# A retention layer and two feed-forward layers on one core: the second tile's state chains merged, rounding and scaled queries moved, two units' loads taken ahead of weights

## The chip, the core and the metric

The kernel runs on 1 core of a Trainium2 chip. The metric is the device time of one execution in microseconds (us). A core has five engines with a queue each: TensorE (PE, its weight load shown apart as PEld), VectorE (DVE), ScalarE (ACT), GpSimd (POOL) and SyncE (SP). Here SP issues nearly all loads; DMAs that add onto their destination are issued by POOL.

## What is computed

```python
def _attn_ref(q, k, v):                      # q, k, v: (2, 8, 768, 64)
    B, H, S, D = q.shape
    gamma = 1.0 - 2.0 ** (-5.0 - np.arange(H, dtype=np.float32))
    scale = 1.0 / np.sqrt(D)
    state = np.zeros((B, H, D, D), dtype=np.float32)
    for t in range(S):
        state = gamma[None, :, None, None] * state + np.einsum('bhd,bhe->bhde', k[:, :, t], v[:, :, t])
        y[:, :, t] = scale * np.einsum('bhd,bhde->bhe', q[:, :, t], state)

def reference(**kwargs):
    x = attn_out.transpose(0, 2, 1, 3).reshape(B * S, H * D)     # 1536 tokens x 512
    x = ((x @ w_a) * (x @ w_b)) @ w_out                          # d_ff 1536
    h = x @ w_in                                                 # d_ff 2048
    return np.maximum(0.01 * h, h) @ moe2_w_out
```

All results are float32. Batch 2, 8 heads, 768 steps, head size 64.

## The kernel before, in words

**Retention.** The 1536 tokens are three tiles of 512. A unit is one tile with one pair of heads, so there are 12 units: 0 to 3 are the first tile, 4 to 7 the second, 8 to 11 the third. Units 0 to 3 work in chunks of 128 steps (the `wide_` functions), the others in chunks of 64, eight to a unit (`subs`). A unit u loads its four tiles n, v (plain k and v) and q, k (transposed). ACT scales n into kd (`scaled_keys`, L584); POOL scales q into qs (`scaled_queries`, L589). PE forms kv per chunk (`states`, L592) and the scores sc (L627); DVE masks sc into P (`masked`, L649) and adds kv chunk by chunk onto the decaying state (`add`, L604): one small instruction per chunk, each of which reads the last one's result. PE then makes x from P and v (`within`) and from qs and the states (`across`). A sequence of 768 steps has 12 chunks of 64, so the second tile holds the last four chunks of one sequence and the first four of the next; the second chain starts with a plain copy (L607) and does not read the first.

**Weights.** They arrive as 64-bit words of 512 KB per 128 rows (`raw_`). ACT begins a rounding in three steps (`begin_steps`, L308 to L312), DVE ends it in three (`round_steps`, L326 to L330). Each rounded float32 tile is split into a high part (ACT, `a0h`) and a low part (DVE subtraction, `a0l`, L961 or L385), and each product of two matrices takes three matmuls (`mm3`, L257 to L259): high by high, high by low, low by high. For each later a-weight the low part is instead made by an ACT multiplication by -1 and a POOL DMA that adds the rounded tile (L382, L383).

**Order.** Every engine runs its own queue strictly in the order in which the source calls it; nothing reorders it. The loop over u (L1021) issues for each u: PE's `states(u + 1)` with `within(u)`, `scores(u + 1)` with `across(u)`, then `FILL[u]` blocks of the first feed-forward layer (`first_blocks`, L964, products pa and pb of weights a0, b0, a1, b1), and between them the DVE, ACT and POOL work. `ROUND` says in which u which weight is rounded, `QUERIES` and `KEYS` in which u scaled queries and keys are issued early, `loads(u + AHEAD)` the loads. `low` (L958) makes the low parts that are pending. `outer` (L983, issued at L1115) is eight DMAs of POOL that add whole tiles xf onto others in two interleaved chains of four; their results feed the casts s10 to s41 (L771).

**Fast blocks.** From f = 2 on, each pair of weight blocks a, b is worked by seven products in place of eight (`seven_for_eight`, L780). It accumulates in a bank named top, from which ACT copies three times (L868, L851, L872) while PE waits to add the next product. Its weights pass through `queue`, which `pump(us)` empties by about so many us at a time. `sub_items` (L400) forms differences of the rounded a and b tiles on DVE.

Of the kernel before, what the change touches and what calls it, by code (L numbers as in the profile page):

```python
# [26 lines left out]
NPAIR = H // 2  # L27
# [17 lines left out]
KEYS = {-1: (2,), 0: (3,), 3: (5,)}  # L45
QUERIES = {5: (7, 8), 6: (9, 10), 7: (11,)}
# [183 lines left out]
def retention_moe_kernel(ctx: ExitStack, tc: tile.TileContext, ins, out):  # L230
# [109 lines left out]
    queue, spare, behind = [], [], []  # L340

# [51 lines left out]
    def enqueue_next(f):  # L393
        for k in "ab":
            enqueue_round()
            enqueue_split((k, f), f in FAST, k == "a")
# [189 lines left out]
    @known  # L586
    def scaled_queries(u, t, p, d):
        d["qs"] = slots.new(F32, f"qs{u}")
        nc.gpsimd.tensor_mul(by_sub(d["qs"]), by_sub(d["q"]), pair_table(p, 0))  # L589

    @known
    def states(u, t, p, d):  # L592

        kv, own, todo = bank(f"kv{u}"), chain[u % 2], []
        d["own"] = [carry[p][t % 2]] + [own[:, m] for m in range(1, SUB)] + [carry[p][(t + 1) % 2]]
        d["adds"] = []
        for m, c in enumerate(subs):
            at0 = (t * SUB + m) % SPB
            if at0 == SPB - 1:
                continue  # L600
            for r in heads:
                todo.append(((kv[r, c], d["kd"][r, c], d["v"][r, c]), (True, True)))

            def add(c=c, m=m, first=not at0):  # L604
                o = d["own"][m + 1]
                if first:
                    nc.vector.tensor_copy(o, kv[:, c])  # L607
                else:
                    nc.vector.scalar_tensor_tensor(
                        o, d["own"][m], small[:, NPAIR + p:NPAIR + p + 1], kv[:, c], op0=ALU.mult, op1=ALU.add  # L610
                    )

            d["adds"].append(add)
        slots.done(1)
        return todo
# [330 lines left out]
    load_weights()  # L946
# [11 lines left out]
    def low():  # L958
        while lows:
            key = lows.pop()  # L960
            nc.vector.tensor_sub(weights[key][1], rounded.pop(key), as32(weights[key][0]))  # L961
            slots.done(1)
# [33 lines left out]
    def rounding(u):  # L996
        weigh(u)
        if ROUND.get(u + 1, (0, 0, 0))[2] > 1:
            begin_weights()
        while done:  # L1000
            high(done.pop())

    def weigh(u):
        if u not in ROUND:
            return
        kind, f, n = ROUND[u]
        if n > 1:
            turn.append(round_steps())
        for _ in range(n):
            next(turn[0], None)  # L1010
        if ROUND.get(u + 1, (0, 0))[:2] != (kind, f):
            for _ in turn.pop():
                pass
            done.append((kind, f))
# [5 lines left out]
    turn = []  # L1020
    for u in range(-1, len(units)):  # L1021
        if u < NPAIR:
# [14 lines left out]
            else:  # L1037
                masked(u + 1)
                weigh(u)
                for step in un[u + 1]["adds"][:3]:  # L1040
                    step()
# [15 lines left out]
            if u == NPAIR - 1:  # L1057
                high(done.pop())
                low()
                for step in un[u + 1]["adds"][3:]:  # L1060
                    step()
                x_low(u)
# [5 lines left out]
        else:  # L1068
# [3 lines left out]
            steps = un[u + 1]["adds"] if u + 1 in un else []  # L1072
            if u == NPAIR:
                weigh(u)
                masked(u + 1)
                for step in steps:
                    step()
                x_high(u)
                keys(u + 2)
                queries(u + 2)  # L1080
                high(done.pop())
                low()
                x_low(u)
                begin_weights()
            else:
                low()
                for step in steps[:3]:
                    step()
                masked(u + 1)
                for step in steps[3:4]:  # L1090
# [5 lines left out]
                for step in steps[4:]:  # L1096
# [8 lines left out]
        loads(u + AHEAD)  # L1105
        if u in (10, 11):
# [48 lines left out]
    for f in range(NBLOCK, FF1):  # L1155
# [26 lines left out]
        if before:  # L1182
            next(before, None)
            make_products(f - 1)
        if f == FAST[-1]:
# [371 lines left out]
```

## Time and profile before

| what | value |
|---|---|
| median of 3 runs | 563.97 us (563.68 to 564.5) |
| the profiled execution's own time | 563.54 us |
| its span | 561.7 us |
| PE busy | 551.4 us, 98% of the span |
| DVE, ACT, POOL busy | 463.3, 386.8, 155.3 us |

The span runs from the first to the last instruction of the profile; the 1.84 us beside it lie around it. The PE's busy time counts a matmul from its start to its modelled end, so a stall shows as PE idle time, and a lower clock shows as longer matmuls under a granted clock below 1.00.

### The profile page before, as it was taken

Reading aid. Unit: us, or ns where it says so; the run is one execution under the profiler, and the core shown is the slowest. Engines: PE = TensorE matmul, PEld = TensorE weight load, DVE = VectorE, ACT = ScalarE, POOL = GpSimd, SP = SyncE. Lnnn points to the kernel's source line nnn. Section 1 sums busy time; section 2 is a strip of 40 time slices with the busy share of each in tenths; the row PEclk is TensorE's granted clock in tenths of the full one; section 3 lists DMA queues with packets and bytes.
Section 4 is the critical chain, followed back from the end, with each engine's and each line's share of the span. In section 5 each row is a group of like instructions: output and inputs, shape, how many; then the busy total and the mean of one; then the engine's idle time right before and its main releaser. Section 6 shows DMA issues by size and latency. Waiting matters only on the chain.

```text
span 561.7 us, 10490 instructions
## 1 busy us (share of the span) xinstructions
PE 551.4 (98%) x3745; PEld 462.8 (82%) x3745; DVE 463.3 (82%) x984; ACT 386.8 (69%) x796; POOL 155.3 (28%) x198
## 2 busy tenths in 40 slices
PE   8899998999999999999999999999999999999997
PEld 5777886888888888888888888888888888888886
DVE  5888966888988898999769887896977798999862
ACT  4865466777887888968747556778766896678800
POOL 2240320113223231157540140221333467600000
PEclk9999999999999999999999999999999999999999
DMA  8994744548887889699993361764677799964111
GB/s 317 394 388 176 144 76 116 145 140 231 229 214 212 252 224 301 197 333 233 248 223 96 57 131 39 215 178 157 194 254 229 213 273 238 226 159 121 57 57 57
DMA packets 50053, 108.78 MB, mean 194 GB/s; under 512 B 5968, under 2 KB 13392, under 8 KB 50000
## 3 DMA queue, kind: packets, MB, share of 16 engines
q1 hardware_dynamic: 27504, 66.86, 35.7%
q0 software_dynamic: 22208, 40.91, 34.1%
q8 instruction: 29, 0.48, 0.3%
q10 hardware_dynamic: 288, 0.34, 0.2%
q14 instruction: 24, 0.20, 0.1%
HBM read 74.00 MB, written 18.35 MB: 164 GB/s over the span
## 4 chain that ended last, share of the span: by engine, by line
PE 85%; DMA 10%; ACT 2%; DVE 1%; issue 1%; POOL 0%; SPq 0%; POOLq 0%
PE blk L258 12%; PE blk L257 12%; PE blk L259 12%; PE top L257 5%; PE top L258 5%; PE top L259 5%; DMA xf<-xf 3%; PE pa L259 3%; PE pa L257 3%; PE pa L258 3%; PE pb L259 3%; PE pb L258 3%; PE pb L257 3%; PE mid L257 3%; PE mid L258 3%; PE mid L259 3%
## 5 line engine op out<-in xcount | busy, mean ns | idle before, releaser
L258 PE MATMUL blk<-form,form 128*128 128x512 f32 (+1 forms) x224 | 75.8, 339 | 0.0
L257 PE MATMUL blk<-form,form 128*128 128x512 f32 (+1 forms) x224 | 75.6, 337 | 0.0
L259 PE MATMUL blk<-form,form 128*128 128x512 f32 (+1 forms) x224 | 75.3, 336 | 0.0
L173 DVE TENSOR_TENSOR form<-g,form 128x512 fp32r<-128x512 f32 x112 | 57.7, 553 | 0.9
L258 PE MATMUL blk<-forma,forma 128*128 128x512 f32 (+1 forms) x168 | 56.9, 338 | 0.0
L257 PE MATMUL blk<-forma,forma 128*128 128x512 f32 (+1 forms) x168 | 56.7, 337 | 0.0
L259 PE MATMUL blk<-forma,forma 128*128 128x512 f32 (+1 forms) x168 | 56.4, 336 | 0.0
L167 ACT CAST form<-g 128x512 fp32r<-128x512 f32 x112 | 52.6, 514 | 3.6 <-DMA g<-g 2.2
L173 DVE TENSOR_TENSOR forma<-h,forma 128x512 fp32r<-128x512 f32 x84 | 43.1, 554 | 5.4 <-ACT forma L167 3.9
L257 PEld LDWEIGHTS blk<-form,form 128*128 128x128 f32 x224 | 42.5, 190 | 5.3
L258 PEld LDWEIGHTS blk<-form,form 128*128 128x128 f32 x224 | 42.5, 190 | 4.7
L259 PEld LDWEIGHTS blk<-form,form 128*128 128x128 f32 x224 | 42.3, 189 | 4.7
L167 ACT CAST forma<-h 128x512 fp32r<-128x512 f32 x84 | 38.9, 512 | 6.5 <-DMA h<-h 6.1
L728 POOL DMA_DIRECT2D farg<-g x26 | 15.7, 617 | 82.4 <-ACT g L1299 62.2
L146 POOL DMA_DIRECT2D h<-h x33 | 32.6, 1161 | 16.4 <-DVE h L858 5.1
L257 PEld LDWEIGHTS blk<-forma,forma 128*128 128x128 f32 x168 | 31.9, 190 | 4.0
L258 PEld LDWEIGHTS blk<-forma,forma 128*128 128x128 f32 x168 | 31.9, 190 | 3.6
L259 PEld LDWEIGHTS blk<-forma,forma 128*128 128x128 f32 x168 | 31.7, 189 | 3.6
L173 DVE TENSOR_TENSOR form<-wq,form 128x256 fp32r<-128x256 f32 x56 | 23.5, 420 | 10.0 <-ACT form L167 9.9
L728 POOL DMA_DIRECT2D farh<-h x19 | 11.0, 576 | 73.5 <-DVE h L858 36.9
L167 ACT CAST form<-wq 128x256 fp32r<-128x256 f32 x56 | 22.7, 405 | 7.4 <-PE blk L258 2.5
L146 POOL DMA_DIRECT2D g<-farg x22 | 22.0, 1059 | 7.2 <-DVE form L173 3.4
(3059 smaller groups left out, 1687.1 us busy)
## 6 DMA issues: line engine op xcount, KB each, us to landing
raw_wi<-in_w SPq DMA_DIRECT2D x16, 512.0 KB, 4.2
raw_wq<-in_w SPq DMA_DIRECT2D x16, 512.0 KB, 5.3
farg<-g POOLq DMA_DIRECT2D x26, 256.0 KB, 3.9
g<-farg SPq DMA_DIRECT2D x26, 256.0 KB, 6.6
raw_a<-in_wab SPq DMA_DIRECT2D x12, 512.0 KB, 5.0
raw_b<-in_wab SPq DMA_DIRECT2D x12, 512.0 KB, 5.3
raw_wo<-in_wo SPq DMA_DIRECT2D x12, 512.0 KB, 5.1
g<-farg POOLq DMA_DIRECT2D x20, 256.0 KB, 8.0
```

The source lines that it names most:

```text
L146: queue.append((0.0, lambda piece=piece: self.nc.gpsimd.dma_start(self.A(*d[1:], j)[piece], self.A(*x1[1:], j)[piece], accum_op=ALU.add)))
L167: nc.scalar.copy(h, src)
L173: nc.vector.tensor_sub(*todo.pop(0))
L257: nc.tensor.matmul(ps, w[0], x[0], start=first, stop=False, skip_group_check=more)
L258: nc.tensor.matmul(ps, w[0], x[1], start=False, stop=False, skip_group_check=more)
L259: nc.tensor.matmul(ps, w[1], x[0], start=False, stop=last, skip_group_check=more)
L728: nc.gpsimd.dma_start(self.far[t, f], self.tiles[t, f])
```

## The change

What it does, part by part:

1. Loads: the weight tile that stood ahead of each of units 5 and 6 on SP's queue, and likewise of unit 7, now stands behind that unit's four loads.
2. States of the second tile (units 4 to 7): the chunk steps 1 and 2 of both chains are one instruction each (`both`, 128x2x64), seven instructions become five; for units 6 and 7 the copy that starts the second chain moves from DVE to ACT.
3. Around unit 4 the whole chain is done ahead of the mask, and the rounding of weight a0 behind it; the rounding of b0 moves behind unit 5's chain; the low parts of x03 and x20 move ahead of those of a0 and b0.
4. Unit 5: kd5 moves up on ACT between the first and the second step that begin a0; qs5 is made by DVE in the midst of the rounding of a0, no longer by POOL.
5. Each later query scaling on POOL waits for the last low part that was issued ahead of it (a0l, b0l, a1l, b1l), and units 8 and 10 are one u later in `QUERIES`.
6. The low part of a2 is a DVE subtraction, no longer an ACT step and a POOL DMA; so the eight sums `outer` are the first DMAs on POOL.
7. At the first fast block `pump(2.0)` runs the roundings of a3 and b3 ahead of the copies out of top and left.

```diff
-KEYS = {-1: (2,), 0: (3,), 3: (5,)}
-QUERIES = {5: (7, 8), 6: (9, 10), 7: (11,)}
+KEYS = {-1: (2,), 0: (3,)}
+QUERIES = {5: (7,), 6: (8, 9), 7: (10, 11)}
...
-            enqueue_split((k, f), f in FAST, k == "a")
+            enqueue_split((k, f), f in FAST, k == "a" and f in FAST[1:])
...
     def scaled_queries(u, t, p, d):
         d["qs"] = slots.new(F32, f"qs{u}")
-        nc.gpsimd.tensor_mul(by_sub(d["qs"]), by_sub(d["q"]), pair_table(p, 0))
+        args = by_sub(d["qs"]), by_sub(d["q"]), pair_table(p, 0)
+        if u == NPAIR + 1:
+            nc.vector.tensor_mul(*args)
+            return
+        made = nc.gpsimd.tensor_mul(*args)
+        if behind_low:
+            tc.add_manual_dep(
+                made.ins, behind_low[-1].ins.name,
+                mybir.DependencyInfo(mybir.DependencyClass.Sync, mybir.DependencyReason.DATA),
+            )
...
     def states(u, t, p, d):
...
+        def one(m):
+            add(d["own"][m + 1], d["own"][m], of[:, m])
+
+        def both(m):
+            add(own[:, m + 1::fresh][:, :2], own[:, m::fresh][:, :2], of[:, m::fresh][:, :2])
+
+        fresh = -t * SUB % SPB
+        if fresh < SUB:
+            copy = nc.vector.tensor_copy if u < NPAIR + 2 else nc.scalar.copy
+            d["copy"] = lambda: copy(own[:, fresh + 1], of[:, fresh])
+            todo_adds = [lambda: one(0)]
+            todo_adds += [lambda m=m: both(m) for m in range(1, fresh - 1)]
+            todo_adds += [lambda m=m: one(m) for m in range(2 * fresh - 1, SUB)]
+        else:
+            d["copy"] = lambda: None
+            todo_adds = [lambda m=m: one(m) for m in range(SPB - 1 - t * SUB % SPB)]
...
     loads(4)
     load_weights()
-    load_weights()
     loads(5)
     load_weights()
     loads(6)
...
         while lows:
             key = lows.pop()
-            nc.vector.tensor_sub(weights[key][1], rounded.pop(key), as32(weights[key][0]))
+            behind_low.append(
+                nc.vector.tensor_sub(weights[key][1], rounded.pop(key), as32(weights[key][0]))
+            )
...
     def rounding(u):
         weigh(u)
         if ROUND.get(u + 1, (0, 0, 0))[2] > 1:
-            begin_weights()
+            for n, _ in enumerate(begin_steps()):
+                if not n and u == NPAIR - 2:
+                    keys(NPAIR + 1)
...
             else:
+                un[u + 1]["copy"]()
+                for step in un[u + 1]["adds"]:
+                    step()
                 masked(u + 1)
-                weigh(u)
-                for step in un[u + 1]["adds"][:3]:
-                    step()
+                rounds = weigh_steps(u)
+                next(rounds)
+                next(rounds)
+                queries(NPAIR + 1)
+                next(rounds, None)
...
             if u == NPAIR - 1:
                 high(done.pop())
+                x_low(u)
                 low()
-                for step in un[u + 1]["adds"][3:]:
-                    step()
-                x_low(u)
                 begin_weights()
...
+            mid = len(steps) // 2
+            if steps and u > NPAIR:
+                un[u + 1]["copy"]()
             if u == NPAIR:
-                weigh(u)
                 masked(u + 1)
+                un[u + 1]["copy"]()
                 for step in steps:
                     step()
                 x_high(u)
                 keys(u + 2)
                 queries(u + 2)
+                weigh(u)
                 high(done.pop())
+                x_low(u)
                 low()
-                x_low(u)
                 begin_weights()
...
         loads(u + AHEAD)
+        if u < 0:
+            load_weights()
...
         if before:
             next(before, None)
             make_products(f - 1)
+        else:
+            pump(2.0)
```

PE's order is unchanged, instruction by instruction. In the rows below a name's first number is the unit or the weight (kv4, a0), the numbers behind it are buffers.

VectorE, unit 4 and weight a0, before:

```order
L651 TENSOR_TENSOR P4_73_462<-sc4_445,second_76 128x512
L326 TENSOR_SCALAR a0_68_408<-a0_68_408 128x512
L328 TENSOR_SCALAR a0_68_408<-a0_68_408 128x512
L330 ISA a0_68_408<-a0_68_408,sl0_409 128x1024
L609 SCALAR_TENSOR_TENSOR cr0_85<-ca01_78,second_76,kv4_430 128x64
L609 SCALAR_TENSOR_TENSOR cr0_85<-cr0_85,second_76,kv4_430 128x64 x2
L961 TENSOR_TENSOR a0l_79_486<-a0_68_408,a0h_78_485 128x512
L607 COPY cr0_85<-kv4_430 128x64
L609 SCALAR_TENSOR_TENSOR cr0_85<-cr0_85,second_76,kv4_430 128x64 x2
L609 SCALAR_TENSOR_TENSOR ca00_77<-cr0_85,second_76,kv4_430 128x64
L662 TENSOR_TENSOR x03l_75_479<-x3_421,x03h_74_478 128x512
```

and now:

```order
L625 COPY cr0_85<-kv4_432 128x64
L614 SCALAR_TENSOR_TENSOR cr0_85<-ca01_78,second_76,kv4_432 128x64
L614 SCALAR_TENSOR_TENSOR cr0_85<-cr0_85,second_76,kv4_432 128x2x64 x2
L614 SCALAR_TENSOR_TENSOR ca00_77<-cr0_85,second_76,kv4_432 128x64
L670 TENSOR_TENSOR P4_74_469<-sc4_447,second_76 128x512
L326 TENSOR_SCALAR a0_68_408<-a0_68_408 128x512
L328 TENSOR_SCALAR a0_68_408<-a0_68_408 128x512
L592 TENSOR_TENSOR qs5_75_473<-q5_23_158,second_76 128x512
L330 ISA a0_68_408<-a0_68_408,sl0_409 128x1024
L681 TENSOR_TENSOR x03l_77_485<-x3_423,x03h_76_484 128x512
L980 TENSOR_TENSOR a0l_79_488<-a0_68_408,a0h_78_487 128x512
```

The chain of unit 4 (cr0, ca00) now stands whole ahead of the mask P4, in five instructions; qs5 is new, inside the rounding of a0, and x03l stands ahead of a0l.

SyncE, the loads of units 5 and 6 (n, v, q, k) and the weight tiles, before:

```order
L287 DMA raw_a0_152<-in_wab 128x512
L287 DMA raw_b0_154<-in_wab 128x512
L507 DMA n5_21_156<-in_kn 128x512
L507 DMA v5_22_158<-in_vn 128x512
L507 DMA q5_23_160<-in_qT 128x512
L507 DMA k5_24_162<-in_kT 128x512
L287 DMA raw_a1_164<-in_wab 128x512
L507 DMA n6_25_166<-in_kn 128x512
L507 DMA v6_26_168<-in_vn 128x512
L507 DMA q6_27_170<-in_qT 128x512
L507 DMA k6_28_172<-in_kT 128x512
```

and now:

```order
L287 DMA raw_a0_152<-in_wab 128x512
L508 DMA n5_21_154<-in_kn 128x512
L508 DMA v5_22_156<-in_vn 128x512
L508 DMA q5_23_158<-in_qT 128x512
L508 DMA k5_24_160<-in_kT 128x512
L287 DMA raw_b0_162<-in_wab 128x512
L508 DMA n6_25_164<-in_kn 128x512
L508 DMA v6_26_166<-in_vn 128x512
L508 DMA q6_27_168<-in_qT 128x512
L508 DMA k6_28_170<-in_kT 128x512
```

raw_b0 stands behind unit 5 and raw_a1 behind unit 6.

ScalarE at the first fast block, around the first copy out of top (h02), before:

```order
L868 COPY h02_165_1414<-top_1424 128x512
L308 ACTIVATE a3_168_1439<-raw_a3_727 128x512
L310 ACTIVATE sl6_1440<-raw_a3_727 128x512
L312 ACTIVATE sl6_1440<-raw_a3_727 128x512
L308 ACTIVATE b3_169_1449<-raw_b3_825 128x512
L310 ACTIVATE sl7_1450<-raw_b3_825 128x512
L312 ACTIVATE sl7_1450<-raw_b3_825 128x512
L693 COPY h12_166_1415<-pa_1417 128x256
```

and now:

```order
L714 ACTIVATE h11_164_1401<-pa11_1284 128x256
L308 ACTIVATE a3_168_1415<-raw_a3_719 128x512
L310 ACTIVATE sl6_1416<-raw_a3_719 128x512
L312 ACTIVATE sl6_1416<-raw_a3_719 128x512
L308 ACTIVATE b3_169_1425<-raw_b3_815 128x512
L310 ACTIVATE sl7_1426<-raw_b3_815 128x512
L312 ACTIVATE sl7_1426<-raw_b3_815 128x512
L887 COPY h02_165_1405<-top_1431 128x512
```

The six steps that begin a3 and b3 stand ahead of the copy of top into h02, behind the copy out of pa11.

## Rows read from the trace of the kernel before

**Rows 1.** The page's busy times: us (share of the span) and instructions.
```profile
PE 551.4 (98%) x3745; PEld 462.8 (82%) x3745; DVE 463.3 (82%) x984; ACT 386.8 (69%) x796; POOL 155.3 (28%) x198
```

**Rows 2.** Stretches: start:end, length, busy us (count) of each engine, PE clock, DMA, GB/s.
```profile
25.50:28.90 3.40, 3.38 (x64) 2.98 (x65) 3.12 (x9) 2.10 (x5) 0.65 (x1) 0.51 1.05 393
60.00:80.00 20.00, 20.00 (x258) 16.58 (x257) 15.45 (x35) 7.85 (x15) 6.88 (x8) 1.00 0.70 120
100.00:500.00 400.00, 399.86 (x1955) 337.71 (x1954) 343.36 (x720) 296.18 (x608) 130.08 (x168) 1.00 0.77 203
500.00:561.70 61.70, 58.20 (x334) 50.96 (x332) 43.46 (x96) 28.92 (x75) 0.87 (x1) 1.00 0.23 73
```

**Rows 3.** PE in order of time, 21 to 43 us: start, us, what [idle before <- releaser].
```profile
21.45 0.88 PE L578 MATMUL x<-qs,wk 128*64 128x128 f32 x12
23.86 0.27 PE L645 MATMUL kv<-v,kd 64*64 64x64 f32 x2 [1.54 <-ACT kd L584]
...
25.52 0.37 PE L645 MATMUL sc<-qs,k 64*64 64x64 f32 x2 [0.49 <-POOL qs L589]
...
27.42 0.79 PE L257 MATMUL pa<-x00h,a0h 128*128 128x512 f32 x1
...
31.02 0.27 PE L645 MATMUL kv<-v,kd 64*64 64x64 f32 x2
...
34.36 0.51 PE L259 MATMUL pb<-x00h,b0l 128*128 128x512 f32 x1 [0.70 <-DVE b0l L961]
...
42.48 0.50 PE L259 MATMUL pa<-x00h,a1l 128*128 128x512 f32 x1 [0.24 <-DVE a1l L961]
```

**Rows 4.** The chain that ended last, in order of time: start, us, what.
```profile
14.57 7.49 DMA raw_b<-in_wab
...
60.14 5.17 DMA xf<-xf
...
87.73 3.58 DMA a3l<-a
```

**Rows 5.** ACT in order of time, 20.8 to 23.8 us.
```profile
20.81 0.67 ACT L308 ACTIVATE a<-raw_a 128x512 f32<-128x512 f32 x1
...
22.63 0.56 ACT L657 CAST x03h<-x 128x512 fp32r<-128x512 f32 x1
23.09 0.72 ACT L584 ACTIVATE kd<-n,second 128x512 f32<-128x512 f32 x1
```

**Rows 6.** DVE in order of time: mask P4, chain of unit 4, a0l, b0l.
```profile
21.57 0.69 DVE L651 TENSOR_TENSOR P<-sc,second 128x512 f32<-128x512 f32 x1 [1.40 <-PE sc L645]
...
23.81 0.28 DVE L609 SCALAR_TENSOR_TENSOR cr<-ca,second,kv 128x64 f32<-128x64 f32 x1
24.12 0.60 DVE L609 SCALAR_TENSOR_TENSOR cr<-cr,second,kv 128x64 f32<-128x64 f32 x2
24.64 1.38 DVE L961 TENSOR_TENSOR a0l<-a,a0h 128x512 fp32r<-128x512 f32 x1
...
32.62 1.69 DVE L961 TENSOR_TENSOR b0l<-b,b0h 128x512 fp32r<-128x512 f32 x1
```

**Rows 7.** POOL in order of time: qs5, the DMA for a2l, the last of the outer sums.
```profile
24.18 1.28 POOL L589 TENSOR_TENSOR qs<-q,second 128x512 f32<-128x512 f32 x1 [3.96 <-DMA q<-in_qT]
...
58.88 1.05 POOL L383 DMA_DIRECT2D a2l<-a  x1 [13.05 <-PE kv L645]
...
76.57 0.86 POOL L1115 DMA_DIRECT2D xf<-xf  x1 [2.37 <-DMA xf<-xf]
```

**Rows 8.** ACT at the first fast block: the first copy out of top.
```profile
81.46 0.61 ACT L868 COPY h<-top 128x512 f32<-128x512 f32 x1
```

**Rows 9.** PE at the first fast block: the three products added onto top.
```profile
83.31 0.39 PE L257 MATMUL top<-s20h,tb2h 128*128 128x512 f32 x1
...
87.96 0.50 PE L257 MATMUL top<-s30h,tb2h 128*128 128x512 f32 x1 [0.41 <-ACT u L851]
...
94.38 0.50 PE L257 MATMUL top<-x22h,ta2h 128*128 128x512 f32 x1 [1.84 <-ACT h L872]
```

More of the change, by code (lines that the diff above doesn't have):

```diff
@@ L340, in retention_moe_kernel @@
     queue, spare, behind = [], [], []
+    behind_low = []
     def pump(us):
@@ L595, in states, with add @@
         d["own"] = [carry[p][t % 2]] + [own[:, m] for m in range(1, SUB)] + [carry[p][(t + 1) % 2]]
-        d["adds"] = []
         for m, c in enumerate(subs):
[L598 to L613, printed above, removed]
+            if (t * SUB + m) % SPB < SPB - 1:
+                for r in heads:
+                    todo.append(((kv[r, c], d["kd"][r, c], d["v"][r, c]), (True, True)))
+        of = by_sub(kv)
+        fall = small[:, NPAIR + p:NPAIR + p + 1]
+        def add(o, old, part):
+            nc.vector.scalar_tensor_tensor(o, old, fall, part, op0=ALU.mult, op1=ALU.add)
+        def one(m):
[12 more added lines that the diff above has]
+            todo_adds = [lambda m=m: one(m) for m in range(SPB - 1 - t * SUB % SPB)]
+        d["adds"] = todo_adds
         slots.done(1)
@@ L998, in rounding, with weigh_steps @@
         if ROUND.get(u + 1, (0, 0, 0))[2] > 1:
-            begin_weights()
+            for n, _ in enumerate(begin_steps()):
+                if not n and u == NPAIR - 2:
+                    keys(NPAIR + 1)
         while done:
             high(done.pop())
+    def weigh_steps(u):
+        if u in ROUND:
+            yield from round_steps()
+            done.append(ROUND[u][:2])
     def weigh(u):
[L1004 to L1014, printed above, removed]
+        for _ in weigh_steps(u):
+            pass
     def fill(u):
@@ L1018, in fill @@
             next(dense)
-    turn = []
     for u in range(-1, len(units)):
@@ L1086, in retention_moe_kernel @@
                 low()
-                for step in steps[:3]:
+                for step in steps[:mid]:
                     step()
                 masked(u + 1)
-                for step in steps[3:4]:
+                for step in steps[mid:mid + 1]:
                     step()
@@ L1095, in retention_moe_kernel @@
                 leave_x(u)
-                for step in steps[4:]:
+                for step in steps[mid + 1:]:
                     step()
```

## The prediction

> **What bounds the kernel now.** I read the page's busy times first. PE is busy for 551.4 of 561.7 us [rows 1], so some 10.3 us is all that PE's waits can give back, apart from a low clock. The table of stretches tells where they are: from 100 to 500 us PE idles 0.14 us in 400, and 3.5 us lie in the tail, where outputs leave [rows 2]. The change touches neither. What it can win lies ahead of 100 us, and PE's own order is unchanged there, so the time is the sum of PE's waits and slow stretches. PE in order of time shows them [rows 3]: 1.54 us until kd5 is there, 0.49 until qs5, 0.70 until b0l, 0.24 until a1l. At the first fast block it waits 0.41 us for ACT's second copy out of top and 1.84 for the third [rows 9]. [...] Together: 1.54 + 0.49 + 1.67 + 0.70 + 0.24 + 0.41 + 1.84 = 6.89 us.
>
> **From unit 4 to the first block (before: PE runs from 22.33, where 21.45 + 0.88 ends, to 31.02, where unit 6's states begin [rows 3]).** I rebuild this stretch from durations of rows.
>
> Loads. The queue moves about 390 GB/s here [rows 2], so 256 KB take 0.67 us. raw_b0 lands at 14.57 + 7.49 = 22.06 [rows 4], n5 0.67 behind it at 22.7. With raw_b0 moved behind unit 5, its four tiles land two such steps (1.34 us) earlier: n5 at 21.4, v5 22.1, q5 at 22.8 in place of 24.18, when POOL begins qs5 [rows 7]. raw_b0 lands some 2.7 us later, at 24.8. If the order of issue did not carry through to landing, n5 would stay at 22.7; that is the far bound, 1.3 us worse, and I take the near one, since the queue is full throughout.
>
> kd5. ACT began it at 23.09, behind the three steps for a0 (20.81 to 22.63, so 0.6 each) and x03h [rows 5]. Now it stands behind the first step: 21.4 to 22.1.
>
> P4 and the chain. The mask began at 21.57, the chain only 2.24 us later [rows 6]; now the chain is first. The kv4 group is complete before the 32 score matmuls that end at 21.45; these take about 1.0 (half of the 1.90 us from 25.52 to 27.42 at half clock [rows 3]), so the chain starts near 20.5. A 64-wide step is 0.31 (23.81 to 24.12). The two-chain step of 128 elements is in no row: at least 0.31, at most the 0.62 of two; a 512-wide mask of 0.69 against 0.28 for 64 gives 0.06 more for 64 more elements, so I take 0.37 and the chain is 3 x 0.31 + 2 x 0.37 = 1.67, to 22.2. P4 (0.69) is there at 22.9. PE waits 0.55 in place of 1.54.
>
> qs5. After P4 come two of the three rounding steps (three were 2.24 - 0.61 = 1.63 us, two about 1.0), then qs5 on DVE. POOL took 1.28 [rows 7]; DVE's 128x512 product of the same shape takes 0.69 [rows 6], so it ends near 24.5. PE finishes states and first products 1.15 us after 22.9 and waits 0.45 for it, as against 0.49.
>
> a0. Its last step ends at 25.1, a0h (ACT, about 0.6) at 25.7, a0l at 26.4. That low part took 1.38 us while POOL scaled qs5 from 24.18 on, and b0l 1.69 [rows 6]; I take 0.69 for both, as POOL now waits for them. PE's scores end at 25.5; it waits 0.2 for a0h and 0.2 for a0l, and does the 12 matmuls of pa in 2.8 (18 matmuls from 83.31 to 87.55 are 0.235 each [rows 9]): 28.7.
>
> kd6 is the new wait. Behind a0h ACT has three steps for b0 (1.82), two copies of about 0.5 and kd6 (0.72): 29.2. PE waits 0.5.
>
> So unit 6 begins at 29.2 in place of 31.02: waits of 0.55 + 0.45 + 0.4 + 0.5 = 1.9 replace 1.54 + 0.49 + 1.67 = 3.7, **a gain of 1.8 us**. It rests on the upper clock; see the rivals.
>
> **b0l and a1l.** DVE after a0l: P5 0.61, chain 1.67, rounding of b0 1.63: 30.3. b0h 30.9, b0l 31.6. PE needs it two groups of 1.0 and two matmuls after 29.2, at 31.8. **The 0.70 goes**, with 0.2 to spare. Then DVE stands: unit 6's chain now needs a copy by ACT, queued behind the steps of a1 (30.9 + 1.82) and a tile copy: about 33.5. From there chain, P6, x21l, a product and the rounding of a1 are 4.8 us, a1h 0.6 and a1l 0.69: 39.6. PE needs it at 42.24 - 2.5 = 39.7. **The 0.24 goes** as well, but its cover is 0.1 us; 0.5 us later on ACT and PE waits 0.4.
>
> POOL's queries now wait for low parts. q6 lands six steps of 0.67 behind q5 (k5, raw_b0 for two, n6, v6, q6), at 26.8, after a0l; qs6 is there at 28.1, PE asks for it at 30.2, so it has 2 us to spare. While POOL works, DVE runs mask and chain, which read one operand from PSUM: the chain at 24.12 kept 0.30 a step beside qs5 [rows 6, 7].
>
> **First fast block.** Before, POOL's a2l DMA goes out at 58.88 and the eight sums behind it; the last is issued at 76.57 [rows 7], with 5.17 us a link [rows 4], and ACT can copy top into h02 only at 81.46 [rows 8], after casts that wait for them. Everything behind is late: a3l's DMA goes out at 87.73 and takes 3.58 [rows 4], then DVE's differences and ACT's third copy, which PE awaits until 94.38. Now POOL is free of queries near 47 (qs10 and qs11 behind b1l) and four links end near 68, some 12 us earlier. DVE pays 0.69 for a2l, ACT saves about as much; DVE is busy for 15.45 of the 20 us from 60 to 80 [rows 2], which hides it.
>
> In exchange the copy into h02 stands behind two weights' steps (2 x 1.82). From the end of pa11 PE has 27 matmuls (6.3 us) to the first product that adds onto top (83.31 before); ACT has two half-width copies (about 0.5), the steps 3.64 and the copy 0.61, 4.75 in all: 1.5 us to spare. With PE 2.7 earlier it wants the third copy at 94.38 - 1.84 - 0.41 - 2.74 = 89.4; a3l's DMA can go out by 81, land at 84.6, and differences (four, 1.8) and casts bring the copy to about 88. **0.41 + 1.84 = 2.25 us go.**
>
> **Sum.** 1.8 + 0.70 + 0.24 + 2.25 = 4.99: the profiled 563.54 becomes 558.5. The median of the runs is 0.43 above the profiled run, so **559.0 us** is predicted. From 100 us on PE's load is unchanged, so the lead is kept.
>
> **Rivals.**
> *The clock falls again.* The new waits (0.55, 0.45, 0.4, 0.5) are shorter but closer together. The stretch from 24.5 would again be at 0.51 and cost 1.6, of which the waits for a0 (0.4) and kd6 (0.5) are swallowed: 0.7 worse, 559.7. For it: the clock fell after 2.03 us of idling in pieces. Against: 0.70 at 34.36 and 1.84 at 94.38 did not lower it [rows 3, 9]. [...]
> *The fast block keeps its wait.* The six steps ahead of h02, or a3l's DMA, are later than I set them: 2.25 us come back, 561.2. The spare 1.4 to 1.5 us speaks against it.
> *ACT's copy for unit 6 delays a1.* DVE stands 1.9 us for it; each us beyond costs PE one, up to about 1.5: 560.5.
> *The loads do not come earlier.* They share one full queue: n5 at 22.7, 1.3 us worse, 560.3.
> *Slower: PE stays at the lower clock.* If the frequent short waits keep it there from 24.5 past unit 6's states, 8 to 9 us of full-clock work take twice as long: -5.0 + 8.5 less 0.9 of swallowed waits is +2.6, 566.6. It decides once the low stretch holds over 7 us of such work. Against it: the clock came back after 3.4 us with dense matmuls under way.
>
> **How the numbers follow.** A measurement of this kernel can tell about 0.2%, 1.1 us, from no change. Chances: forecast 0.50, clock 0.18, fast block 0.12, ACT's copy 0.08, loads 0.05, slower 0.04; 0.03 for several of the small losses together, which leaves a time within the 0.2%. All but the last two are faster by over 0.2%; as two losses can meet in the others, I give 0.90 faster, 0.06 same, 0.04 slower. The low end is all 6.89 us less the 0.55 and 0.45 that the chain sets: 558.1, and 0.4 for shorter waits: 557.7. The high end takes in the fast-block rival with 0.4 for a1: 561.6.
>
> **What would show it.** Right: kd5 at about 21.4; unit 6's states near 29.2 with a clock of 1.00 from 24 to 29; a0l and b0l at 0.69; no PE wait at b0l; the eight sums from 47 to 68; no PE wait of over 0.3 at the first fast block. Wrong: a stretch at 0.51 after 24; PE waiting for POOL's qs6 or qs8, for ACT's copy into h02, or for a1l.

## The result, and the profile after

The changed kernel takes **558.6 us** in the median of 6 runs (557.6 to 561.08), the kernel before 563.83 beside it on the same chip (6 runs): ratio 0.9912, interval 0.989 to 0.9934. Run again later it took 558.11 against 563.88, ratio 0.9907 (0.9887 to 0.9927). The forecast was 559.0, with a range of 557.7 to 561.6. The profiled execution took 557.6 us, the shortest of the six; its span is 555.8.

The page's line of busy times (us, share of the span, instructions), against [rows 1], and its chain that ended last by engine:

```profile
PE 549.5 (99%) x3745; PEld 462.3 (83%) x3745; DVE 458.8 (83%) x976; ACT 385.9 (69%) x797; POOL 152.7 (27%) x196
...
PE 95%; DMA 2%; ACT 1%; DVE 1%; issue 0%; POOL 0%; SPq 0%
```

PE's waits in the whole span of the changed kernel (us in total, times, longest); everything behind the first line is 1.3 us. Of the four waits of [rows 3] one is left, at the matmul that waited for qs5 (`sc L664 <- issue`, 0.29 us where it was 0.49; e9's row for the same matmul names DVE's qs); the two of [rows 9] are gone:

```profile
PE warm L957 <- DVE warm L948: 1.2, 1, 1.2
PE sc L534 <- DMA k<-in_kT: 0.3, 1, 0.3
PE sc L664 <- issue: 0.3, 1, 0.3
PE pb L259 <- issue: 0.3, 1, 0.3
PE x L664 <- DVE P L670: 0.2, 1, 0.2
PE sc L534 <- DVE qs L527: 0.2, 1, 0.2
```

Stretches, with the columns of [rows 2]. The granted clock is 1.00 where it was 0.51 before; PE does not idle from 60 to 80 us, and from 100 to 500 us it is as busy as it was:

```profile
22.40:24.50 2.10, 1.90 (x72) 1.60 (x68) 2.03 (x6) 2.10 (x4) 0.00 (x0) 1.00 1.04 394
24.50:27.90 3.40, 3.05 (x72) 2.23 (x69) 3.28 (x8) 2.45 (x6) 0.40 (x1) 1.00 1.05 394
...
60.00:80.00 20.00, 20.00 (x258) 16.60 (x257) 16.96 (x35) 11.29 (x22) 2.58 (x3) 1.00 0.39 78
...
100.00:500.00 400.00, 399.90 (x1964) 338.41 (x1964) 345.01 (x726) 300.09 (x620) 129.57 (x167) 1.00 0.77 201
```

PE in order of time, for [rows 3] and [rows 9]. Where before it stood for kd5, qs5, b0l, a1l and the copies out of top, two short waits are left around unit 5, at 23.52 and 24.96; the one at 46.34 is new:

```profile
23.00 0.33 PE L664 MATMUL kv<-v,kd 64*64 64x64 f32 x4
23.52 0.27 PE L664 MATMUL x<-P,v 64*64 64x64 f32 x2 [0.20 <-DVE P L670]
...
24.96 0.27 PE L664 MATMUL sc<-qs,k 64*64 64x64 f32 x2 [0.29 <-issue]
...
29.58 0.27 PE L664 MATMUL kv<-v,kd 64*64 64x64 f32 x2
...
32.07 0.40 PE L259 MATMUL pb<-x00h,b0l 128*128 128x512 f32 x1
...
39.70 0.39 PE L259 MATMUL pa<-x00h,a1l 128*128 128x512 f32 x1
...
45.69 0.39 PE L258 MATMUL pb<-x00l,b1h 128*128 128x512 f32 x1
46.34 0.39 PE L259 MATMUL pb<-x00h,b1l 128*128 128x512 f32 x1 [0.27 <-issue]
...
80.73 0.39 PE L257 MATMUL top<-s20h,tb2h 128*128 128x512 f32 x1
...
84.81 0.39 PE L257 MATMUL top<-s30h,tb2h 128*128 128x512 f32 x1
...
88.66 0.39 PE L259 MATMUL pa<-x11h,a3l 128*128 128x512 f32 x1
88.89 0.39 PE L257 MATMUL top<-x22h,ta2h 128*128 128x512 f32 x1
```

DVE in order of time, for [rows 6]: the chain stands ahead of P4, its two pair steps take 0.73 together, and the low parts take 0.69, not 1.38 and 1.69:

```profile
21.52 0.27 DVE L614 SCALAR_TENSOR_TENSOR cr<-ca,second,kv 128x64 f32<-128x64 f32 x1
21.82 0.73 DVE L614 SCALAR_TENSOR_TENSOR cr<-cr,second,kv 128x128 f32<-128x128 f32 x2
22.59 0.28 DVE L614 SCALAR_TENSOR_TENSOR ca<-cr,second,kv 128x64 f32<-128x64 f32 x1
22.78 0.68 DVE L670 TENSOR_TENSOR P<-sc,second 128x512 f32<-128x512 f32 x1
...
26.15 0.69 DVE L980 TENSOR_TENSOR a0l<-a,a0h 128x512 fp32r<-128x512 f32 x1
...
31.16 0.69 DVE L980 TENSOR_TENSOR b0l<-b,b0h 128x512 fp32r<-128x512 f32 x1
33.59 0.28 DVE L614 SCALAR_TENSOR_TENSOR cr<-ca,second,kv 128x64 f32<-128x64 f32 x1 [1.74 <-ACT cr L625]
```

ACT and POOL in order of time, for [rows 5], [rows 7] and [rows 8]: the eight sums are issued from 47.56 to 63.70 and the first copy out of top runs at 79.02:

```profile
22.09 0.72 ACT L585 ACTIVATE kd<-n,second 128x512 f32<-128x512 f32 x1
...
79.02 0.57 ACT L887 COPY h<-top 128x512 f32<-128x512 f32 x1
...
87.81 0.58 ACT L891 COPY h<-top 128x512 f32<-128x512 f32 x1
```

```profile
47.56 1.90 POOL L1141 DMA_DIRECT2D xf<-xf  x2
...
63.70 0.86 POOL L1141 DMA_DIRECT2D xf<-xf  x1 [0.69 <-DMA xf<-xf]
81.06 0.86 POOL L384 DMA_DIRECT2D a3l<-a  x1 [16.50 <-PE pa L259]
```

**Where the time went.** PE's order is the same in all kernels, so the starts of four of its matmuls cut each span into five parts: kv4 (unit 4's states), b1l (the first product with b1l), s20 and x22 (first and third product onto top). In us, from PE's rows in order of time of each profiled execution; the last column goes by the span, which the page gives to 0.1:

| kernel | kv4 at | kv4 to b1l | b1l to s20 | s20 to x22 | x22 to end |
|---|---|---|---|---|---|
| before | 19.56 | 29.27 | 34.48 | 11.07 | 467.4 |
| changed | 20.29 | 26.05 | 34.39 | 8.16 | 466.9 |
| changed, again (e5) | 19.57 | 27.29 | 34.53 | 8.16 | 466.9 |
| e1 | 20.78 | 25.83 | 37.07 | 8.83 | 467.3 |
| e2 | 20.95 | 25.85 | 34.41 | 10.67 | 467.3 |
| e3 | 19.41 | 27.89 | 34.39 | 8.16 | 466.9 |
| e4 | 19.97 | 27.34 | 35.62 | 8.16 | 467.0 |
| e6 | 19.26 | 28.23 | 34.54 | 8.16 | 466.9 |
| e7 | 19.98 | 25.61 | 35.40 | 10.41 | 467.4 |
| e8 | 20.44 | 28.50 | 34.54 | 8.16 | 466.9 |
| e9 | 19.95 | 27.85 | 34.40 | 8.16 | 467.0 |
| e10 | 20.82 | 28.26 | 34.39 | 8.16 | 467.0 |
| e11 | 21.08 | 26.01 | 34.41 | 8.16 | 467.1 |
| e12 | 21.26 | 25.63 | 35.20 | 8.16 | 467.0 |

Of the 5.9 us between the spans of before and changed, 3.22 come from kv4 to b1l, 2.91 from the first fast block and 0.4 after it; a later start took 0.73 back. In the second execution the first of these is only 1.98.

### The profile page after: what moved, and what is told of

Same layout as the page of the kernel before. It is cut to its first block, busy times and chain, and to the rows that moved or that the text cites. A ratio compares the mean times of both kernels' runs of the same rounds, so it can differ in the third digit from the quotient of the medians.

```text
span 555.8 us, 10480 instructions
## 1 busy us (share of the span) xinstructions
PE 549.5 (99%) x3745; PEld 462.3 (83%) x3745; DVE 458.8 (83%) x976; ACT 385.9 (69%) x797; POOL 152.7 (27%) x196
## 4 chain that ended last, share of the span: by engine, by line
PE 95%; DMA 2%; ACT 1%; DVE 1%; issue 0%; POOL 0%; SPq 0%
PE blk L258 12%; PE blk L257 12%; PE blk L259 12%; PE top L257 5%; PE top L258 5%; PE top L259 5%; PE pa L257 4%; PE pb L257 4%; PE pb L259 4%; PE pb L258 4%; PE pa L259 4%; PE pa L258 4%; PE mid L257 3%; PE mid L259 3%; PE mid L258 3%; DMA n<-in_kn 2%
## 5 line engine op out<-in xcount | busy, mean ns | idle before, releaser
L167 ACT CAST forma<-wo 128x256 fp32r<-128x256 f32 x42 | 16.8, 401 | 11.4 <-PE blk L259 11.4
```

The source lines that it names most:

```text
L167: nc.scalar.copy(h, src)
```

## The experiments

All are the changed kernel, edited as shown, except e8 (the kernel before with two edits); each ran beside the kernel before on the same chip.

**e1: GpSimd keeps the differences of its first tensor a.**

```diff
-            enqueue_split((k, f), f in FAST, k == "a" and f in FAST[1:])
+            enqueue_split((k, f), f in FAST, k == "a")
```

> The changed kernel, but the low part of a2 is again an ACT step and a POOL DMA ahead of the eight sums; the rest, the pumped roundings too, as changed. Theory (the sums lead, so the first fast block's waits go): the a2 DMA can go out only near 55 us, so the sums run from 56 to 76 in place of 47 to 66; ACT's last casts end near 77, the six steps of a3 and b3 and the copy into h02 near 82.5 where TensorE asks for it at 80.3: TensorE waits some 2 us there, in all 2 to 3.5 us over the changed kernel, 560.6 to 562.1. Rival (the pumped roundings carry this part of the gain): no new wait, 558.6 to 559.1.

Measured: 559.41 us (558.97 to 561.66), ratio 0.9934 (0.9917 to 0.9951), some 0.8 to 1.3 us above the changed kernel. a2l's DMA goes out at 55.47, the eight sums from 56.18 to 74.55, and the wait is at the first product onto top:

```profile
83.68 0.50 PE L257 MATMUL top<-s20h,tb2h 128*128 128x512 f32 x1 [2.50 <-ACT h L887]
```

So the wait is where the theory put it. The profiled execution was the slowest of the six, so it shows the place better than the size: the median lies between the theory's 560.6 to 562.1 and the rival's 558.6 to 559.1, and the interval overlaps the changed kernel's.

**e2: no roundings pumped behind them.**

```diff
-        else:
-            pump(2.0)
```

> The changed kernel without the pumped roundings at the first fast block, the sums still lead. Theory (the sums carry the gain, the pumped roundings the rest): h02 is copied at once, the steps of a3 begin some 3 us later, its DMA goes out near 83, and the third copy out of top is there about 90 where TensorE asks for it at 89.2: a wait of 0.5 to 1.2 us, 559.1 to 559.8. Rival (the pumped roundings carry it all): the 0.41 and 1.84 us waits of before return, 560.9. Second rival (they do nothing): 558.6.

Measured: 561.18 us (559.59 to 564.46, 12 runs), ratio 0.9962 (0.9944 to 0.9979). The sums run as in the changed kernel (48.22 to 63.75), yet the third copy out of top is as late as before:

```profile
91.88 0.50 PE L257 MATMUL top<-x22h,ta2h 128*128 128x512 f32 x1 [1.83 <-ACT h L891]
```

The rival's size stood, but part of that is luck: one wait of the two is back, and in 5 of the 12 executions the mean clock is 0.997 (median 562.74 us); the other seven have a median of 560.61.

So without the pumped roundings the third copy is late although the sums lead. The wait for the second copy is gone here, but e7 shows below that it is gone without either edit too.

**e3: the loads where they were before.**

```diff
+    load_weights()
     loads(5)
...
-        if u < 0:
-            load_weights()
```

> The changed kernel with the loads of weights in their old places, so that n5 to k5 land 1.34 us later. Theory (landing follows the order of issue): kd5 starts 1.3 us later on ACT and holds up the other steps of a0; TensorE waits about 1 us more ahead of unit 5, of which the later waits for qs5 and kd6 swallow part: 0.5 to 1.0 us slower, 559.1 to 559.6, and 0.7 more if the clock falls there. Rival (the loads share one full queue and it makes no difference): 558.6, within 0.3.

Measured: 558.57 us (558.18 to 559.17), ratio 0.9912 (0.9897 to 0.9927): no difference in time that can be told. In the trace PE waits for kd5 again,

```profile
23.36 0.27 PE L664 MATMUL kv<-v,kd 64*64 64x64 f32 x2 [1.17 <-ACT kd L585]
```

and unit 4 to unit 6 takes 10.04 us where it took 9.29. Two things hide it: the wait at b1l (0.90 here) and the start. kv4 began at 19.26 to 20.44 in the four executions with the loads of before (before, e3, e6, e8; mean 19.67) and at 19.57 to 21.08 in the seven with moved loads and the same start-up (changed, e1, e2, e4, e5, e7, e11; mean 20.37). Whether the moved loads cost those 0.7 us at the start, or it is chance, so few executions don't settle.

**e4: GpSimd's queries free of the low parts.**

```diff
-        if behind_low:
+        if False:
```

> The changed kernel without the wait of GpSimd's query scalings for low parts; their order on GpSimd is the same. Theory (what they cost is the low part beside them): qs7 starts when q7 has landed, about 31.7, beside b0l, qs8 and qs9 at 36 beside the rounding of a1; b0l takes 1.2 to 1.7 in place of 0.69 and TensorE waits 0.3 to 0.8 us for it: 0.3 to 1.0 us slower, 558.9 to 559.6. Rival (the queries land late enough to miss the low parts now): 558.6, within 0.2, and b0l and a1l stay at 0.69.

Measured: 558.85 us (557.95 to 559.86), ratio 0.9918 (0.9904 to 0.9932). GpSimd's qs9 runs from 38.22 to 39.51 and meets DVE's a1l:

```profile
38.73 1.33 DVE L980 TENSOR_TENSOR a1l<-a,a1h 128x512 fp32r<-128x512 f32 x1 [0.69 <-ACT a1h L973]
```

```profile
40.12 0.50 PE L259 MATMUL pa<-x00h,a1l 128*128 128x512 f32 x1 [0.31 <-DVE a1l L980]
```

The whole is 0.3 to 0.7 us longer than the changed kernel, within what the intervals leave open. b0l was not late: pb<-x00h,b0l starts at 31.74, 0.23 behind the matmul before it.

**e5: the changed kernel again**, as a control in another session.

> The changed kernel itself, timed again beside the next three, as their measure. All theories: 558.6, within 0.5; TensorE's start of unit 4's states between 19.4 and 21 us, by how the first loads land.

Measured: 558.11 us (557.44 to 560.91). Nearly all as before, but PE waits 1.06 us at b1l, where it had waited 0.27, and the row names a releaser that has nothing to do with it:

```profile
46.86 0.40 PE L259 MATMUL pb<-x00h,b1l 128*128 128x512 f32 x1 [1.06 <-DVE cr L614]
```

**e6: unit 4 as before, with the merged steps kept** (loads, kd5, POOL's qs5, the order of mask, rounding and chain, a0l ahead of x03l).

```diff
-KEYS = {-1: (2,), 0: (3,)}
+KEYS = {-1: (2,), 0: (3,), 3: (5,)}
...
-            nc.vector.tensor_mul(*args)
+            nc.gpsimd.tensor_mul(*args)
...
+                masked(u + 1)
+                weigh(u)
                 un[u + 1]["copy"]()
...
-                masked(u + 1)
-                rounds = weigh_steps(u)
...
-                queries(NPAIR + 1)
...
```

> The changed kernel with all that it changes around units 4 and 5 undone: loads and kd5 in their old places, qs5 by GpSimd without a wait, mask and rounding of a0 ahead of the chain, a0l ahead of x03l; the merged steps, unit 5's order and later are kept. Theory (this part is worth 1.8 us, of which 1.67 is the clock): TensorE waits 1.5 and 0.5 us again, the granted clock falls to about 0.5 from 25.5 to 29, and from the start of unit 4's states to that of unit 6's it takes 11.5 us in place of 9.3: 2.0 us slower, some 560.6. Rival (the clock fell by chance or for another reason): clock 1.00 throughout, 0.5 us slower, 559.1. Second rival (later waits swallow what this part wins): 558.6 in spite of the low clock.

Measured: 558.75 us (557.98 to 559.12), ratio 0.9912 (0.9895 to 0.9928). In the profiled execution the waits for kd5 and qs5 are back (1.61, 0.58), the clock falls as before, and unit 4 to unit 6 takes 11.70 us, 2.4 more than in the changed kernel:

```profile
25.50:28.90 3.40, 3.40 (x64) 2.99 (x65) 2.50 (x7) 2.44 (x5) 0.79 (x1) 0.50 1.05 393
```

By b1l the difference is 2.18 us to the changed kernel's first execution and 0.94 to its second: where PE comes later it does not wait there (in e6 b1l starts at 47.49). The profiled start is also the earliest of all (19.26). In the time, 0.15 to 0.6 us are left, where the theory told 2.0. But only the profiled one of the four executions has a low mean clock (0.997, 558.87 us); the others have 0.999 or 1.000, at 557.98 to 559.12. So the time of e6 says little on what a fall of the clock costs.

**e7: both edits at the fast block undone** (those of e1 and e2).

> The changed kernel without both edits of the first fast block: a2's low part by GpSimd's DMA again, no pumped roundings. Theory (the parts add): the early gain of 2.7 us stays, the waits of 0.4 and 1.8 us at the first fast block return: 560.9. Rival (each of the two edits covers for the other, so that without both more is lost than 2.25): TensorE comes 2.7 us earlier to a wait whose end is set by the sums on GpSimd, which start some 4 us earlier: waits of 2 to 4 us there, 561 to 563. Second rival: the sums start early enough with GpSimd's queries alone, 559.

Measured: 560.58 us (560.17 to 562.6), ratio 0.9955 (0.9937 to 0.9973). So all edits before 50 us give about 2.5 us alone. Of the two waits of [rows 9] only the third copy's is back:

```profile
85.07 0.39 PE L257 MATMUL top<-s30h,tb2h 128*128 128x512 f32 x1
...
91.40 0.50 PE L257 MATMUL top<-x22h,ta2h 128*128 128x512 f32 x1 [1.83 <-ACT h L891]
```

The eight sums run from 55.38 to 70.82 here, some 4 to 6 us earlier than before, as GpSimd's DMA for a2l goes out at 54.66 and not at 58.88; with that the first copy out of top runs at 78.47 in place of 81.46, and the second is in time. a3l's DMA goes out at 84.72, as in e2 (84.94), against 81.06 in the changed kernel. So in these profiles the low part of a2 on VectorE wins nothing at the fast block without the pumped roundings; with them it takes away the wait that e1 shows.

**e8: the kernel before with these two edits alone.**

> The kernel before with the two edits of the first fast block alone: a2's low part on VectorE and the pumped roundings. Theory (the parts add): the sums start near 51 in place of 59.6, the waits of 0.41 and 1.84 us go, all else stays: 2.25 us faster than before, 561.3 by this chip's 563.5. Rival (these edits pay only when TensorE arrives early): no gain, 563.5. Second rival (the copy into h02 behind six steps makes a wait): slower than before.

Measured: 560.4 us (559.73 to 561.0), ratio 0.9943 (0.9929 to 0.9958): 3.2 us. The two parts add up within the intervals, 0.45% and 0.57% against 0.88 to 0.93% for the whole. In this profile PE waits for kd5 as before (1.43 us) but only 0.17 for qs5, and the clock holds:

```profile
25.50:28.90 3.40, 3.23 (x84) 2.57 (x75) 3.26 (x9) 2.54 (x5) 1.01 (x2) 1.00 1.06 397
```

**The wait at b1l.** In four executions PE stood at the same matmul, pb<-x00h,b1l, with 851 matmuls and 852 weight loads before it: 0.27 us (changed), 1.06 (e5), 0.90 (e3), 0.67 (e4). b1l itself was there: DVE ended it at 44.93 in the changed kernel, and the weight load of the same product ran from 45.69 to 45.88. What does fit is a packet of the queue named "instruction". The page counts 29 such packets with 0.48 MB for the 7,490 matmuls and weight loads of PE, one for every 258; and one of them stands alone in the stretch from 44.1 to 44.2 us of the changed kernel (packets, MB, share of 16 engines: 0.96 us of one engine):

```profile
q8 instruction: 29, 0.48, 0.4%
```

```profile
q8 instruction: 1, 0.02, 60.1%
```

PE goes on 2.2 to 2.6 us after such a packet begins. Two theories were set against each other: PE lacks its next instructions there (then the place is fixed by the count of instructions), or it waits for data. e9, e10 and e12 change the start-up matmuls, whose results nothing reads.

**e9: 20 more instructions at the start.**

```diff
-    keep_warm(NWARM)
+    keep_warm(NWARM - 10)
+    for _ in range(20):
+        nc.tensor.matmul(wps[:, 0:TT // 2], warm[:, 0:P], warm[:, 0:TT // 2], start=True, stop=True)
```

> The ten start-up matmuls of 512 columns become twenty of 256 columns: the same columns, but 20 more instructions (10 matmuls, 10 weight loads) ahead of all later TensorE work. What it tells apart is the wait at the matmul pb<-x00h,b1l (0.27, 1.06, 0.90 and 0.67 us in four profiled executions, each time with 851 matmuls before it, 2.2 to 2.6 us after a 16 KB packet on the instruction queue q8 began). Code theory: TensorE waits there for its next instructions; the place is fixed by the count of instructions, so it moves 10 matmuls ahead, to the last two small matmuls before pa<-x22h,a0h, and pb<-x00h,b1l starts without a wait; the wait at the new place may be anything from 0 to 1.1 us. Data theory: that matmul waits for a result of another engine (the profile names VectorE's cr once and issue once); the wait stays at pb<-x00h,b1l, 0.3 to 1.1 us. Time: within 0.8 us of the changed kernel's 558.1 to 558.6 by either.

Measured: 559.75 us (558.17 to 562.69), ratio 0.9924 (0.99 to 0.9947). The wait moved exactly 10 matmuls ahead, in front of the last pair of small ones, and b1l starts on the beat:

```profile
43.71 0.22 PE L664 MATMUL x<-qs,cr 64*64 64x64 f32 x2
45.65 0.27 PE L664 MATMUL sc<-qs,k 64*64 64x64 f32 x2 [1.72 <-issue]
45.85 0.50 PE L257 MATMUL pa<-x22h,a0h 128*128 128x512 f32 x1
...
47.80 0.40 PE L259 MATMUL pb<-x00h,b1l 128*128 128x512 f32 x1
```

Again 851 matmuls stand before it. It is longer there, as PE comes to it 2.1 us sooner (at 43.93, not 46.07) while the packet begins only 0.9 us sooner. The data theory falls. The time was missed: 559.75 lies 1.2 to 1.6 us above the changed kernel's, where 0.8 was allowed for, though the intervals overlap.

**e10: 60 more instructions.** As e9, with forty matmuls of 128 columns in place of the ten of 512.

> As the run before, but the ten start-up matmuls become forty of 128 columns: 60 more instructions (30 matmuls, 30 weight loads). Code theory: the place moves 30 matmuls ahead, into the small 64x64 matmuls of unit 11, near 43.5 us; pb<-x00h,b1l starts without a wait, and if the small matmuls wait, then by up to 1.1 us there. Data theory: the wait stays at pb<-x00h,b1l, 0.3 to 1.1 us. Time: within 0.8 us of the changed kernel's 558.1 to 558.6 by either; below 557.9 only if the packet is no longer waited for anywhere.

Measured: 562.38 us (560.38 to 562.95), ratio 0.9968 (0.9955 to 0.9981): nearly 4 us worse than the changed kernel, where 0.8 was allowed for. b1l does not wait, but the end of a packet two before it now falls right behind a run of small matmuls, with 597 matmuls and 598 weight loads before it:

```profile
34.66 0.39 PE L257 MATMUL pb<-x00h,b0h 128*128 128x512 f32 x1 [2.47 <-ACT cr L625]
```

The packet began at 32.2, 2.5 us before. The trace also holds the semaphore instructions of PE's queue, 22 before this place and 26 before b1l's; with them it is 1217 instructions here and 1729 there, 512 apart, which is two packets if one holds 256; the page gives one for every 258 matmuls and weight loads. The code theory holds for the place; I had thought only of the one boundary. It also shows that the releaser in such a row can be a bystander. The profiled execution is the shortest of the eight (560.38); where the median loses 2 us more was not seen, but 5 of the eight have a mean clock of 0.997.

**e11: the pair steps apart again.**

```diff
-            add(own[:, m + 1::fresh][:, :2], own[:, m::fresh][:, :2], of[:, m::fresh][:, :2])
+            one(m)
+            one(m + fresh)
```

> The second tile's state steps one by one again (no pair of 64-column steps in one instruction, three copies on VectorE), all else as changed. By the prediction's sum: four pair steps at 0.37 become eight steps at 0.31, of which the chain of unit 4 carries two more instructions, so P4 and the first across matmuls come 0.4 us later (x<-P of unit 4 waits 0.6 in place of 0.2 us), the distance from kv4 to kv6 grows from 9.3 to 9.7 us, and the time by 0 to 0.4 us, 0 if the wait near 46 us takes it up as it took up the late unit 4. Rival: the pair steps matter later too, VectorE being 83% busy, and the low parts b0l and a1l come late again: over 0.6 us.

Measured: 560.03 us (558.57 to 562.41), ratio 0.9928 (0.9904 to 0.9952); the interval overlaps the changed kernel's, so the time stays unclear. The edit undoes the pair steps only: the copies of units 6 and 7 stayed on ACT (34.38 and 40.35 us), though the expectation says three copies on VectorE, so what that move is worth was not tried. Unit 4 to unit 6 takes 9.41 us, 0.12 more than with pairs (0.4 was expected), PE waits 0.3 in place of 0.2 us for P4, and neither b0l nor a1l is late. The single executions lie at 558.6 (three) and 561.3 to 562.4 (three); the profiled one is of the first kind, and what the others lost was not seen.

**e12: 236 more instructions, 20 short of 256.** As e9, with 128 matmuls of 64 columns.

> The ten start-up matmuls of 512 columns become 128 of 64 columns on 64 weight columns: 236 more instructions, that is 20 fewer than one block of 256. Code theory, now with the run of 20 more instructions behind it (its wait, 1.7 us, came 10 matmuls ahead, as told): the block's end then lies 10 large matmuls behind pb<-x00h,b1l, TensorE comes to it 2.3 us later, and no wait is left there or at pb<-x00h,b1l; b1l's matmul starts 26.1 us after kv4 where it started 26.05 to 27.9 us after it; time 557.4 to 558.4, at or just under the changed kernel's 558.1 to 558.6. If the count of instructions doesn't matter, the wait of 0.3 to 1.1 us is at pb<-x00h,b1l again. A shorter or colder start-up is a risk of this edit: then kv4 starts later than 20.3 us or the clock of the first 20 us falls below 1.00, and the time says nothing.

Measured: 559.08 us (557.55 to 560.06) against 564.35, ratio 0.9904 (0.9885 to 0.9923). b1l starts 25.63 us after kv4 (26.1 was told), without a wait, the least of all kernels but e7; yet kv4 starts at 21.26, and from b1l to s20 0.8 us are lost, with waits of 0.18 and 0.24 at 52.42 and 58.04 and the rest in gaps too short to be shown as waits. These two waits fit the code theory: counted as in e10, 2241 and 2497 instructions stand before them, two and three times 256 more than 1729, and a packet began 2.9 and 2.2 us before. The time is 0.7 us above what was told; as kv4 started later than 20.3, it says nothing by the expectation's own condition. The ratio is the lowest of all and cannot be told from the changed kernel's. No run beat it by more than its interval.

Taken together, the changed kernel's wait, every wait on "issue" of 0.4 us or more behind 30 us, and the four rows with a bystander (e5, e3, e4, e10), end alike; "count" is the number of PE's instructions before the place, semaphore instructions included:

| kernel | count | packet begins | PE goes on | idle shown |
|---|---|---|---|---|
| changed, e5 | 1729, 1729 | 44.1, 44.4 | 46.34, 46.86 | 0.27, 1.06 |
| e3, e4 | 1729, 1729 | 44.7, 44.7 | 47.30, 47.31 | 0.90, 0.67 |
| e4, e7 | 1985, 1985 | 49.7, 48.2 | 52.11, 50.68 | 0.46, 0.73 |
| e9, e10 | 1729, 1217 | 43.2, 32.2 | 45.65, 34.66 | 1.72, 2.47 |

All counts lie whole multiples of 256 apart. In the changed kernel PE had passed the place 256 instructions earlier, 1473, at 42.06; the packet began 2.1 us later, and PE ran the 256 instructions between in 4.0 us, which is less than the 2.1 + 2.2 us until it could go on.

The 16 DMA engines are busy for 0.99 of the time up to 46.34 us in the changed kernel. Whether a packet would begin sooner under a lighter load is not shown: no such run was made.

## Why the prediction was right, and where its steps were not

*Loads, kd5, chain.* Right. kv4 started 0.73 us later than in the execution before; set off by that, kd5 was told for 22.1 and began at 22.09. A pair step was put at 0.37 and takes 0.36 (0.73 for two). e11 shows that the merging as such is worth little, 0.12 us of stage.

*Unit 4 to unit 6.* A gain of 1.8 was told; by the trace it is 2.17 (11.46 less 9.29). The rows show less idle time than the four new waits that were told: P4 0.20 for 0.55, qs5 0.29 for 0.45, and none for a0h and a0l (0.4) and kd6 (0.5). That is 0.49 for 1.9, yet the stage is only 0.37 shorter than told, because a wait costs more than the idle time that its row shows: from the last start before it to the next it is 0.41 for P4 and 0.51 for qs5, and 0.50 ahead of unit 6's states, where it was 0.32 in the kernel before.

*The clock.* It stayed at 1.00, so the first rival did not come true. The 1.67 us in the sum, 3.40 x 0.49 by the stretch at 0.51 [rows 2], are an estimate of mine: no run shows this term. They were also mis-sized as a gain over the median, as not every execution before has the low stretch. One such stretch takes 3.40 x 0.49 / 561.7 = 0.003 off the mean clock. Of 52 timed executions of the kernel before, 19 have 0.999 or 1.000 (median 563.26 us), 26 have 0.996 or 0.997, as one stretch gives (564.3), and seven have 0.993 or 0.994, as two would (563.85). So executions that lost as much as one stretch are 1.0 us longer, and those that lost twice as much are 0.6 longer: what a fall costs is not settled by these, and none shows 1.67. Nor is its place: e6 and e8, with the waits of unit 4 as before, have a low mean clock in 2 of 9 executions, e2 and e7, which of the long waits before keep only the 1.83 us at the third product, in 6 of 18. The prediction held, from one execution, that the 1.84 us there did not lower the clock; it may do so in others. All 12 of the changed kernel have 0.999 or 1.000.

*b0l and a1l.* Right. b0l ended at 31.85 and was wanted at 32.07 (0.22 to spare, told 0.2); a1l at 39.40 for 39.70 (0.3, told 0.1). DVE stood 1.74 us for ACT's copy, told 1.9. The price of meeting GpSimd was read right: 1.33 against 0.69 in e4.

*What was not foreseen* is that part of this early gain is given back at b1l, 0.27 in one execution and 1.06 in the other: from kv4 to b1l 3.22 and 1.98 us were won, for 1.8 + 0.94 = 2.74 told. It is also in part why e6, which loses 2.4 us by unit 6 in its profiled execution, costs little in the end; the clock held in its other three.

*The fast block.* The mechanism was right: the last sum was issued some 13 us earlier (63.70 for 76.57), the first copy out of top came 1.1 us ahead of its need (79.59 for 80.73), the third 0.5 (88.39 for 88.89). The size was off: 2.25 told, 2.91 measured, and 0.4 more behind it that no wait accounts for and that every kernel without one or both of the edits lacks (467.3 to 467.4 against 466.9 to 467.1). The step that failed is to price a wait by its idle time. Before the third product [rows 9] PE's last matmul began at 92.15 and the next at 94.38; on the beat it would have been 0.23, as in the changed kernel (88.66, 88.89), so 2.00 us were lost where 1.84 are shown, and the first interval behind it was 0.33, not 0.22.

```profile
92.15 0.40 PE L259 MATMUL pa<-x11h,a3l 128*128 128x512 f32 x1
```

I had treated sums and roundings as one step. In e1 without the early sums the first product waits, in e2 without the pumped roundings the third, and in e7 without both the third alone: the 0.41 us go with the early edits alone. In e2 the second rival's 561.2 was met by 561.18, but with one wait of the two and the help of a lower clock.

*The sum.* 4.99 was told, 5.2 and 5.8 were measured between medians. The total held in part by luck, because terms erred both ways: in the two profiled executions the early part gave 0.5 more or 0.8 less than told, the fast block and what follows it 1.1 more, and the start was not counted.

## What to carry to other kernels

Price a wait of TensorE by the distance between the starts of its neighbours less their beat, not by the idle time that the row shows: here a wait cost 0.2 to 0.3 us more. When all waits for data are gone from a stretch of short matmuls, look at the instruction queue's packets, and test by shifting the count of instructions: a wait that moves with the count, as it did by 10 matmuls in e9, is not one for data. Compare stages between fixed matmuls of an unchanged order, since the start alone differed by 1.8 us between executions.

## What was not expected of the hardware

TensorE ran out of instructions, by all that the runs show: the waits of the table, 0.27 to 2.47 us, each end 2.2 to 2.6 us after a packet of 16 KB on the instruction queue began (0.48 MB in 29 packets), at places fixed by the count of instructions (e9, e10). These places lie multiples of 256 instructions apart (1217, 1729, 1985), in or behind runs of 64-column matmuls, and the page counts one packet for every 258 matmuls and weight loads.

The fall of the clock is not fixed by the program: e8, with unit 4 as before and waits of 1.43 and 0.17 us, held 1.00 in the profiled execution, e6 with 1.61 and 0.58 fell to 0.50 in its own, and the kernel before fell, by its mean clock, in 33 of 52 executions. What tells these executions apart, no run shows. Where a longer wait is left, the mean clock is low in some executions too: 0.997 in 5 of the 12 of e2 (wait of 1.83) and 5 of the 8 of e10 (2.47); where in the execution it fell, these do not show.
